# Attention over a cached K and V, gated with a small MLP: where gelu is kept, how the last K and V loads are ordered, and the form of the last product

## The chip, the core and the metric

The kernel runs on one core of one Trainium2 chip. Its time is the device time of one execution in microseconds; the figure of a kernel is the median of several runs. Five engines work side by side: TensorE (PE, with its weight loads listed as PEld), VectorE (DVE), ScalarE (ACT), GpSimd (POOL) and SyncE (SP), which here issues nearly all DMA transfers. Sixteen DMA engines move the data from memory (HBM) into the on-chip memory.

## What is computed

One token attends to a cache of 65,536 positions. There are 16 query heads and 8 K/V heads of width 256; two query heads share one K/V head. Beside that a small MLP works on the same input row, and a scalar gate mixes the two. Cut to what matters:

```python
def reference(A_x, A_k_cache, A_v_cache, A_wq, A_wo, B_x, B_w1, B_b1, B_w2, B_b2, gate_w):
    x = A_x                                              # [1, 1, 448], bf16 like all inputs
    g = _sigmoid((x * gate_w).sum(-1, keepdims=True))    # one number
    q = (x @ A_wq) as 16 heads of 256
    scores = q . k * 256 ** -0.5                         # k, v: [8, 65536, 256], each used by 2 heads
    a = softmax(scores) . v, all heads joined (4096) @ A_wo      # [1, 1, 448]
    h = _layernorm(x)
    u = _gelu(h[d] * w1[f] + b1[f])                      # [448, 1792], tanh form
    b = u @ w2 + b2                                      # [448]
    return g * a + (1 - g) * b
```

The caches are 256 MiB each, so 512 MiB have to be read once; wq and wo are 3.5 MiB each.

## The kernel before

**Blocks.** The cache of one K/V head is cut into four blocks of 16,384 positions, which makes 32 blocks, `n` from 0 to 31; `L` is 31. In a block, partition `p` holds 128 consecutive positions (its rows `j`). K lies in two tiles `k_tiles[0]` and `k_tiles[1]` of 64 rows each (4 MiB each), V in one tile `vt` of 128 rows (8 MiB). There is one buffer of each, so a load waits until the data before it has been read.

**One block.** `score_block` (L350) makes 32 steps `t`: four f32 transposes on TensorE (L327), which turn K rows into columns two bf16 at a time, and one copy by DVE (L332) from PSUM into `kT`. Four PSUM tiles `tps` are used in turn. Steps 0 to 15 read the first K tile, 16 to 31 the second; eight groups `i` of four steps each are followed, two and three steps later, by score matmuls (L341). `softmax` (L380) takes the block's maximum, joins it with the running one (L383 to L395), makes the exponentials on ScalarE (L399), the correction factor `al` (L404), transposes the exponentials into `pT` (L407) and updates the running sum `lsum` (L409). `pv_block` (L376) multiplies V by `pT` in 64 matmuls (L367) with 4 columns of `pT` stationary and 512 elements of V moving, and `accumulate` (L415) adds the product to `acc`, scaled by `al`. After four blocks `head_end` (L455) divides, collects `acc` into two columns per head (L439), and projects them with wo (L450) into a row `a_acc`.

**Order.** The helper `seq` chains the instructions of each engine in the order in which the program writes them, so each queue runs in that order. SyncE's queue, which issues the loads: wq, K of block 0, then for each block `n` V of `n` and the two K halves of `n + 1`; wo goes between V of block 0 and K of block 1 (L477). For `n` = 30 (L470) both K halves of block 31 come ahead of V of block 30. In block 31 (L482) the order is: all score steps, then `load_v_last`, then the products of block 30, `accumulate(30)`, `base` (the row of everything but the last head's share, L486), and then the softmax of block 31.

**The small MLP.** `gel`, the 14 x 448 gelu values per partition, lies in a part of `vt` (L100), which V of block 0 fills later. ScalarE writes it (L238); `mixer_tail` (L288), called after step 11 of block 0, reads it with 14 matmuls (L291) and makes `rest`, the MLP's share times one minus the gate. The gate's sum, its exponential and its reciprocal (L246 to L248, L279 to L282) stand ahead of block 0 in the queues of DVE and ScalarE.

**The end.** V of block 31 goes into the K tiles as they come free: `load_v_last` (L121) issues rows 0 to 63, 64 to 95, and then the last 32 rows in four pieces, each of which takes the same columns of two groups of 16 rows (`pairs`). Products of all but the last two columns of these pairs are made in the usual form (L507 to L513) and accumulated, `collect(fst, False)` (L515) gathers them, and the last four rows' products are made with V stationary (L519): 128 x 128 of V as weights, two columns of `pT` moving. Two multiplications by `rdv` (one over the sum) give `oT`, `project` makes the row, one DVE instruction (L528) multiplies by the gate and adds `base`, and one transfer of 896 bytes stores it (L532).

Of the kernel before, what the change touches and what calls it, by code (L numbers as in the profile page):

```python
# [8 lines left out]
FP32 = mybir.dt.float32  # L9
# [14 lines left out]
NI = VP // NJ  # L24
TAIL = 2


@with_exitstack
def kernel(
# [28 lines left out]
    def seq(ins):  # L58
# [40 lines left out]
    wq_t = vt[:, 48:56, :].rearrange("p a b -> p (a b)")  # L99
    gel = vt[:, 56:56 + 25, :].rearrange("p a b -> p (a b)")[:, 0:NF * D].rearrange(  # L100
        "p (b n) -> p b n", b=NF
    )

# [10 lines left out]

    def load_v(n):
        seq(nc.sync.dma_start(out=vt[:, :, :], in_=rows(A_v_cache, n)))

    def pairs(ap):
        return ap.rearrange("p (i j) d -> p i j d", i=2)

    def load_v_last(n):  # L121
        src = rows(A_v_cache, n)
        seq(nc.sync.dma_start(out=k_tiles[0][:, :, :], in_=src[:, 0:KP, :]))
        seq(nc.sync.dma_start(out=k_tiles[1][:, 0:32, :], in_=src[:, KP:KP + 32, :]))
        for j0, j1 in ((0, 8), (8, 12), (12, NJ - TAIL), (NJ - TAIL, NJ)):
            seq(nc.sync.dma_start(
                out=pairs(k_tiles[1][:, 32:64, :])[:, :, j0:j1, :],
                in_=pairs(src[:, KP + 32:VP, :])[:, :, j0:j1, :],
            ))
# [107 lines left out]
    for b in range(NF):  # L237
# [3 lines left out]
        ))  # L241
    zt = work.tile([1, D], FP32)
    z = const.tile([1, 1], FP32)
    ez = const.tile([1, 1], FP32)
    gate = const.tile([1, 1], FP32)
    seq(nc.vector.tensor_tensor(out=zt[:], in0=xf[0:1, :], in1=gw[:], op=ALU.mult))  # L246
    seq(nc.vector.tensor_reduce(out=z[:], in_=zt[:], op=ALU.add, axis=AXIS.X))
    seq(nc.scalar.activation(out=ez[:], in_=z[:], func=ACT.Exp, scale=-1.0))  # L248


# [24 lines left out]
    for i in range(1, NI):  # L275
        seq(nc.vector.tensor_copy(
            out=qpad[:, :, :, i, i * REP:(i + 1) * REP], in_=qpad[:, :, :, 0, 0:REP]
        ))
    seq(nc.vector.tensor_scalar(  # L279
        out=gate[:], in0=ez[:], scalar1=1.0, scalar2=None, op0=ALU.add  # L280
    ))
    seq(nc.vector.reciprocal(out=gate[:], in_=gate[:]))  # L282

    y_sb = const.tile([1, D], FP32)
    b2f = const.tile([1, 1], FP32)
    rest = const.tile([1, D], FP32)

    def mixer_tail():  # L288
        y_ps = hd_ps[0:1, 0:D]
        for b in range(NF):  # L290
            seq(nc.tensor.matmul(  # L291
                y_ps, lhsT=w2b[:, b:b + 1], rhs=gel[:, b, :], start=(b == 0), stop=(b == NF - 1)
            ))
        seq(nc.vector.tensor_copy(out=b2f[:], in_=b2b[:]))
        seq(nc.vector.tensor_scalar(  # L295
            out=y_sb[:], in0=y_ps, scalar1=b2f[0:1, 0:1], scalar2=None, op0=ALU.add
        ))
        seq(nc.vector.tensor_scalar(
            out=rest[:], in0=y_sb[:], scalar1=gate[0:1, 0:1], scalar2=None, op0=ALU.mult
        ))  # L300
        seq(nc.vector.tensor_tensor(out=rest[:], in0=y_sb[:], in1=rest[:], op=ALU.subtract))
# [17 lines left out]
    base = const.tile([1, D], FP32)  # L319
    res = const.tile([1, D], BF16)  # L320
    state = {"t": 0}
# [27 lines left out]

    def score_block(n, between=None):  # L350
        due = []
        for t, (i, quarter) in enumerate((i, q) for i in range(NI) for q in range(4)):
# [3 lines left out]
            if quarter == 3:  # L356
                due.append((t + 2, (i, 0)))
                due.append((t + 3, (i, 1)))
            if between is not None and t == 11:
                between()  # L360
        while due:
            scores(n // NB, *due.pop(0)[1])

    def pv(ip, j0, j1, v, first, final, end=NJ):
        for jj in range(j0, j1):
            grp = jj % 4
            seq(nc.tensor.matmul(  # L367
                pv_ps[32 * grp:32 * grp + 2 * REP, :, :],
                lhsT=pT[:, 32 * jj + 2 * REP * ip:32 * jj + 2 * REP * (ip + 1)],
                rhs=pairs(v)[:, :, jj, :],  # L370
                start=(first and jj < 4),
                stop=(final and jj >= end - 4),
                tile_position=(0, 32 * grp),
            ))

    def pv_block():  # L376
        for ip in range(NI // 2):
            pv(ip, 0, NJ, vt[:, 32 * ip:32 * (ip + 1), :], ip == 0, ip == NI // 2 - 1)

# [85 lines left out]

    L = NBLK - 1
    for n in range(NBLK):
        score_block(n, mixer_tail if n == 0 else None)
        if n < L:
            if n == L - 1:  # L470
                load_k(L, 0)
                load_k(L, 1)
                load_v(n)
            else:
                load_v(n)
                if n == 0:
                    seq(nc.sync.dma_start(  # L477
                        out=wo_sb[:], in_=A_wo.rearrange("(h r2 par) n -> r2 h par n", r2=128, par=2)
                    ))
                load_k(n + 1, 0)  # L480
                load_k(n + 1, 1)
        if n == L:  # L482
            load_v_last(L)
            pv_block()
            accumulate(n - 1)
            seq(nc.vector.scalar_tensor_tensor(  # L486
                out=base[:], in0=a_acc[:], scalar=gate[0:1, 0:1], in1=rest[:],
                op0=ALU.mult, op1=ALU.add,
            ))
        softmax(n)  # L490
        if n < L - 1:
            if n % NB == NB - 1:
                denominators()
            pv_block()
            accumulate(n)
            if n % NB == NB - 1:
                head_end(n // NB)


    seq(nc.vector.tensor_scalar(  # L500
        out=lsv[:], in0=val[:], scalar1=lsum[:, 0:1], scalar2=None, op0=ALU.mult
# [4 lines left out]
    seq(nc.vector.reciprocal(out=rdv[:], in_=hd_ps[:, 456:456 + REP]))  # L506
    for ip in range(2):  # L507
        pv(ip, 0, NJ, k_tiles[0][:, 32 * ip:32 * (ip + 1), :], ip == 0, False)
    pv(2, 0, NJ, k_tiles[1][:, 0:32, :], False, False)
    v_end = k_tiles[1][:, 32:64, :]  # L510
    pv(3, 0, 8, v_end, False, False)
    pv(3, 8, 12, v_end, False, True, NJ - TAIL)
    pv(3, 12, NJ - TAIL, v_end, False, True, NJ - TAIL)  # L513
    accumulate(L)
    collect(fst, False)  # L515
    for jj in range(NJ - TAIL, NJ):
        for e in range(2):
            for c in range(2):
                seq(nc.tensor.matmul(  # L519
                    o_ps[c],  # L520
                    lhsT=pairs(v_end)[:, e, jj, :].rearrange("p (d c) -> p c d", c=2)[:, c, :],
                    rhs=pT[:, 32 * jj + 2 * REP * 3 + REP * e:32 * jj + 2 * REP * 3 + REP * (e + 1)],
                    start=False, stop=(jj == NJ - 1 and e == 1),
                ))
    for c in range(2):
        seq(nc.vector.tensor_tensor(out=oT[:, c, :], in0=o_ps[c], in1=rdv[:], op=ALU.mult))  # L526
    project(HKV - 1)
    seq(nc.vector.scalar_tensor_tensor(  # L528
        out=res[:], in0=hd_ps[0:1, 0:D], scalar=gate[0:1, 0:1], in1=base[:],
        op0=ALU.mult, op1=ALU.add,  # L530
    ))
    seq(nc.sync.dma_start(out=out[0, 0].rearrange("(o n) -> o n", o=1), in_=res[:, :]))  # L532

# [29 lines left out]
```

## Time and profile before

| | |
|---|---|
| median of 3 runs | 1304.83 us (1304.53 to 1305.51) |
| the profiled execution's own time | 1304.43 us |
| its span, first to last instruction | 1302.6 us |
| mean granted TensorE clock | 0.848 of full speed |
| PE busy | 993.0 us (76%), 8553 matmuls |
| DVE busy | 755.6 us (58%) |
| ACT busy | 42.7 us (3%) |
| read from HBM | 544.22 MB, 418 GB/s over the span |

The profile is of one execution. Its page gives busy times, the span in 40 equal slices (busy tenths, clock, DMA share and GB/s), the DMA queues, the chain of work that ended last, the costliest groups of instructions and the DMA issues. From the trace come views of a stretch: windows with busy time per engine, a timeline, and the list of who waited for whom. In a timeline line stand start, duration, engine, source line and operation; in brackets the idle time ahead of it and what ended it. "SPq" is SyncE's queue of DMA issues.

### The profile page before, as it was taken

The page shows a single profiled execution, that of the slowest core. Times are in us where ns is not written, and L with a number is a line of the kernel's source. Part 1 is how long each engine was busy: PE and PEld are TensorE (multiplying, and loading weights), DVE is VectorE, ACT ScalarE, POOL GpSimd, SP SyncE. Part 2 cuts the span into 40 slices and gives each one's busy share as a digit, 9 for nine tenths or more (in the row PEclk, how much of TensorE's full clock was granted, in tenths as well). Part 3 has the DMA queues.
Part 4 walks back from the last instruction along what each step waited for, and adds up shares of the span by engine and source line. Part 5 has one row for each costly group of instructions (what it writes and reads, how often), then busy time and mean ns, then how long its engine had stood idle before and what let it go on. Part 6 is the DMA issues. An engine that isn't in the chain of part 4 may idle for free.

```text
span 1302.6 us, 19720 instructions
## 1 busy us (share of the span) xinstructions
PE 993.0 (76%) x8553; PEld 642.7 (49%) x8553; DVE 755.6 (58%) x1358; ACT 42.7 (3%) x107; POOL 4.2 (0%) x7
## 2 busy tenths in 40 slices
PE   3757787877877877687877787977788776888795
PEld 3434445544445545455544455544455544455562
DVE  3545567655566655566655567654567545566581
ACT  4000000000000000000000000000000000000000
POOL 1000000000000000000000000000000000000000
PEclk9877888978889887888878889887889878889786
DMA  8799999999999999999999999999999999999697
GB/s 371 323 435 445 415 430 430 440 436 424 425 432 432 438 431 434 417 432 434 435 437 425 430 427 433 432 443 422 431 427 431 429 422 437 425 428 430 273 420 291
DMA packets 18079, 545.49 MB, mean 419 GB/s; under 512 B 2117, under 2 KB 4680, under 8 KB 5320
## 3 DMA queue, kind: packets, MB, share of 16 engines
q1 hardware_dynamic: 17554, 544.22, 97.5%
q8 instruction: 67, 1.10, 0.3%
q14 instruction: 20, 0.16, 0.0%
q10 hardware_dynamic: 438, 0.01, 0.0%
HBM read 544.22 MB, written 0.00 MB: 418 GB/s over the span
## 4 chain that ended last, share of the span: by engine, by line
DMA 67%; PE 30%; DVE 2%; ACT 1%; issue 0%; ACTq 0%
DMA kn<-in_A_k_cache_dram 64%; PE tps L327 24%; PE sc_ps L341 6%; DMA kn<-in_A_v_cache_dram 2%; DVE kT L332 1%; DMA b1b<-in_B_b_dram 1%; ACT vt L238 1%; PE hd_ps L291 0%; PE hd_ps L450 0%; ACT L248 0%; PE hd_ps L439 0%; PE sm_ps L439 0%; DVE acc L417 0%; DVE rmax L383 0%; DVE y_sb L295 0%
## 5 line engine op out<-in xcount | busy, mean ns | idle before, releaser
L332 DVE COPY kT<-tps 128x1024 bf16<-128x1024 bf16 x1024 | 648.0, 685 | 184.2 <-PE tps L327 183.3
L327 PE MATMUL tps<-ident_f,kn 128*128 128x128 f32 x4096 | 610.6, 299 | 113.9 <-DMA kn<-in_A_k_cache_dram 107.0
L327 PEld LDWEIGHTS tps<-ident_f,kn 128*128 128x128 f32 x4096 | 493.0, 152 | 236.4 <-DMA kn<-in_A_k_cache_dram 124.1
L367 PE MATMUL pv_ps<-vt,pT 128*4 128x512 bf16 x1984 | 179.1, 540 | 89.7 <-DMA vt<-in_A_v_cache_dram 82.1
L341 PE MATMUL sc_ps<-kT,qpad 128*32 128x512 bf16 x2048 | 202.4, 395 | 26.1 <-DVE kT L332 25.6
L367 PEld LDWEIGHTS <-pT 128*4 128x4 bf16 x2046 | 61.8, 111 | 202.6 <-issue 144.1
L417 DVE SCALAR_TENSOR_TENSOR acc<-acc,al,pv_ps 128x512 f32<-128x512 f32 x24 | 17.9, 748 | 170.9 <-PE pv_ps L367 170.9
L341 PEld LDWEIGHTS <-qpad 128*32 128x32 bf16 x2048 | 52.9, 93 | 109.8 <-issue 101.7
L399 ACT ACTIVATE p_sb<-sc_ps,nb 128x512 bf16<-128x512 f32 x32 | 22.0, 687 | 1228.8 <-DVE nb L395 1228.8
L422 DVE COPY acc<-pv_ps 128x512 f32<-128x512 f32 x8 | 5.5, 692 | 61.7 <-PE pv_ps L367 61.7
L407 DVE STREAM_TRANSPOSE pT<-p_sb 128x512 bf16<-128x512 bf16 x32 | 22.8, 711 | 28.9 <-ACT p_sb L399 28.9
L383 DVE TENSOR_REDUCE rmax<-sc_ps 128x1 f32<-128x512 f32 x32 | 22.1, 691 | 22.8 <-PE sc_ps L341 22.8
L384 PE MATMUL sm_ps<-ident_f,rmax 128*1 128x128 f32 x32 | 8.6, 270 | 26.7 <-DVE rmax L383 26.7
L392 PE MATMUL sm_ps<-mrun,ones_f 1*128 1x2 f32 x64 | 15.2, 304 | 14.2 <-DVE mrun L391 11.7
L384 PEld LDWEIGHTS sm_ps<-ident_f,rmax 128*1 128x1 f32 x32 | 2.5, 79 | 43.1 <-DVE rmax L383 43.1
L392 PEld LDWEIGHTS sm_ps<-mrun,ones_f 1*128 1x128 f32 x64 | 12.4, 240 | 20.3 <-DVE mrun L391 16.3
L395 DVE CUSTOM_DVE_ANT_0 junk<-sm_ps,nval 128x2 f32<-128x2 f32 x32 | 5.1, 159 | 18.1 <-PE sm_ps L392 18.1
L425 PE MATMUL hd_ps<-lsum,same 128*128 128x1 f32 x14 | 3.9, 348 | 13.8 <-DVE lsum L409 13.8
L450 PE MATMUL hd_ps<-wo_sb,oT 128*1 128x448 bf16 x32 | 11.4, 463 | 0.2 <-DVE oT L526 0.2
L425 PEld LDWEIGHTS hd_ps<-lsum,same 128*128 128x128 f32 x14 | 3.3, 293 | 14.4 <-DVE lsum L409 14.4
L385 DVE TENSOR_REDUCE mnew<-sm_ps 1x2 f32<-1x64 f32 x24 | 5.1, 212 | 8.7 <-PE sm_ps L384 8.7
L238 ACT ACTIVATE vt<-h_bc,b1f,w1f 128x448 bf16<-128x448 f32 x14 | 9.2, 747 | 5.6 <-DVE h_bc L233 5.6
(92 smaller groups left out, 107.5 us busy)
## 6 DMA issues: line engine op xcount, KB each, us to landing
kn<-in_A_k_cache_dram SPq DMA_DIRECT2D x63, 4096.0 KB, 26.9
kn<-in_A_k_cache_dram SPq DMA_DIRECT2D x2, 2048.0 KB, 12.6
kn<-in_A_v_cache_dram SPq DMA_DIRECT2D x1, 4096.0 KB, 26.2
wo_sb<-in_A_wo_dram SPq DMA_DIRECT2D x1, 3584.0 KB, 32.3
vt<-in_A_wq_dram SPq DMA_DIRECT2D x1, 3072.0 KB, 10.3
kn<-in_A_v_cache_dram SPq DMA_DIRECT2D x1, 2048.0 KB, 25.7
kn<-in_A_v_cache_dram SPq DMA_DIRECT2D x1, 1024.0 KB, 24.7
vt<-in_A_wq_dram SPq DMA_DIRECT2D x1, 512.0 KB
```

The lines of the kernel that those rows point to most:

```text
L238: seq(nc.scalar.activation(out=gel[:, b, :], in_=h_bc[:], func=ACT.Gelu_apprx_tanh, scale=w1f[:, b:b + 1], bias=b1f[:, b:b + 1],))
L327: seq(nc.tensor.transpose(tp[:, jj * 128:(jj + 1) * 128], k_tiles[i // 4][:, i % 4 * NJ + quarter * 4 + jj, :].bitcast(FP32), ident_f[:, :],))
L332: seq(nc.vector.tensor_copy(out=kT_tiles[i % 2][:, quarter * 4:(quarter + 1) * 4, :, :].rearrange("p j n c -> p (j n c)"), in_=tp[:, :].bi ...
L341: seq(nc.tensor.matmul(sc_ps[32 * a:32 * (a + 1), :], lhsT=qpad[:, c, g, i, :], rhs=kT_tiles[i % 2][:, :, 32 * a:32 * (a + 1), c], start=( ...
L367: seq(nc.tensor.matmul(pv_ps[32 * grp:32 * grp + 2 * REP, :, :], lhsT=pT[:, 32 * jj + 2 * REP * ip:32 * jj + 2 * REP * (ip + 1)], rhs=pair ...
L383: seq(nc.vector.tensor_reduce(out=rmax[:], in_=sc_ps[:, :], op=ALU.max, axis=AXIS.X))
L384: seq(nc.tensor.transpose(sm_ps[0:1, 0:128], rmax[:, 0:1], ident_f[:, :]))
L392: seq(nc.tensor.matmul(sm_ps[:, 128:128 + REP], lhsT=ones_f[0:1, :], rhs=mrun[0:1, :], start=True, stop=True))
L399: seq(nc.scalar.activation(out=p_sb[:, :], in_=sc_ps[:, :], func=ACT.Exp, scale=scale, bias=nb[:, 0:1], accum_out=den[:, 0:1],))
L407: seq(nc.vector.transpose(out=pT[:, :], in_=p_sb[:, :]))
L417: seq(nc.vector.scalar_tensor_tensor(out=acc[:], in0=acc[:], scalar=al[:, 0:1], in1=pv_ps[:, :, :], op0=ALU.mult, op1=ALU.add,))
L450: seq(nc.tensor.matmul(a_ps, lhsT=oT[:, c, r:r + 1], rhs=wo_sb[:, g * REP + r, c, :], start=(r == 0 and c == 0), stop=(r == REP - 1 and c ...
```

## The change

Five things are changed.

1. `gel` lies in a part of `wo_sb` instead of `vt`. wo's load is issued after both K halves of block 1. Within wo, the two rows of a pair are now indexed `c`, as in the same memory order as before.
2. The gate's sum and exponential are made after step 8 of block 0 (`gate_sum`), its reciprocal at the head of `mixer_tail`, and `mixer_tail` is called after step 20 instead of 11.
3. For block 30, SyncE issues V's first half, K's first half of block 31, V's second half, K's second half of block 31.
4. In block 31 the products of block 30, `accumulate`, `base` and a new copy of the gate on all partitions (`gcol`) are made after step 17. `load_v_last` issues rows 0-63, 64-95, 96-111, 112-119, 120-123, 124-127, each contiguous.
5. All 128 rows of the last V are stationary: 256 matmuls with 128 x 128 of V as weights and two columns of `pT` moving, which add to `collect(esc, False)`; `esc` is `al` on the selected rows. The final result is made in columns: 112 partitions by 4, with wo's columns as weights, and `base` added by four f32 matmuls ahead; the gate is multiplied into `rdv`. The store writes 112 pieces of 8 bytes.

```diff
@@ gelu @@
-    gel = vt[:, 56:56 + 25, :].rearrange("p a b -> p (a b)")[:, 0:NF * D].rearrange(
-        "p (b n) -> p b n", b=NF
-    )
+    gel = wo_sb[:].rearrange("p h c n -> p (h c) n")[:, 0:NF, :]
...
+    LAST = ((0, 64), (64, 96), (96, 112), (112, 120), (120, 124), (124, 128))
+
     def load_v_last(n):
-        src = rows(A_v_cache, n)
-        seq(nc.sync.dma_start(out=k_tiles[0][:, :, :], in_=src[:, 0:KP, :]))
-        seq(nc.sync.dma_start(out=k_tiles[1][:, 0:32, :], in_=src[:, KP:KP + 32, :]))
-        for j0, j1 in ((0, 8), (8, 12), (12, NJ - TAIL), (NJ - TAIL, NJ)):
+        for j0, j1 in LAST:
             seq(nc.sync.dma_start(
-                out=pairs(k_tiles[1][:, 32:64, :])[:, :, j0:j1, :],
-                in_=pairs(src[:, KP + 32:VP, :])[:, :, j0:j1, :],
+                out=k_tiles[j0 // KP][:, j0 % KP:(j1 - 1) % KP + 1, :],
+                in_=rows(A_v_cache, n)[:, j0:j1, :],
             ))
...
+    def gate_sum():
+        seq(nc.vector.tensor_tensor(out=zt[:], in0=xf[0:1, :], in1=gw[:], op=ALU.mult))
+        seq(nc.vector.tensor_reduce(out=z[:], in_=zt[:], op=ALU.add, axis=AXIS.X))
+        seq(nc.scalar.activation(out=ez[:], in_=z[:], func=ACT.Exp, scale=-1.0))
...
+    def products(n):
+        pv_block()
+        accumulate(n)
+
+    def project_base():
+        seq(nc.vector.scalar_tensor_tensor(
+            out=base[:], in0=a_acc[:], scalar=gate[0:1, 0:1], in1=rest[:],
+            op0=ALU.mult, op1=ALU.add,
+        ))
+        seq(nc.tensor.matmul(
+            sm_ps[:, 200:201], lhsT=ones_f[0:1, :], rhs=gate[0:1, 0:1], start=True, stop=True
+        ))
+        seq(nc.vector.tensor_copy(out=gcol[:], in_=sm_ps[:, 200:201]))
+
+    def before_last():
+        products(L - 1)
+        project_base()
+
     for n in range(NBLK):
-        score_block(n, mixer_tail if n == 0 else None)
...
+        if n == 0:
+            score_block(n, {8: gate_sum, 20: mixer_tail})
+        elif n < L:
+            score_block(n)
+        else:
+            score_block(n, {17: before_last})
+        if n < L - 1:
+            load_v(n)
+            load_k(n + 1, 0)
+            load_k(n + 1, 1)
+            if n == 0:
+                seq(nc.sync.dma_start(
+                    out=wo_sb[:], in_=A_wo.rearrange("(h p c) n -> p h c n", p=128, c=2)
+                ))
+        elif n == L - 1:
+            load_v(n, 0, KP)
+            load_k(L, 0)
+            load_v(n, KP, VP)
+            load_k(L, 1)
+        else:
+            load_v_last(L)
...
+    f_ps = tps[0][0:D // NCOL, 0:NCOL]
+    for k in range(NCOL):
+        seq(nc.tensor.matmul(
+            f_ps[:, k:k + 1], lhsT=base[0:1, :].rearrange("o (m k) -> o k m", k=NCOL)[:, k, :],
+            rhs=ones_f[0:1, 0:1], start=(k == 0), stop=False, skip_group_check=True,
+        ))
+    seq(nc.vector.tensor_scalar(
+        out=esc[:], in0=fst[:], scalar1=al[:, 0:1], scalar2=None, op0=ALU.mult
+    ))
...
+    collect(esc, False)
+    for j in range(VP):
+        i, jj = divmod(j, NJ)
+        for c in range(2):
+            seq(nc.tensor.matmul(
+                o_ps[c],
+                lhsT=k_tiles[j // KP][:, j % KP, :].rearrange("p (d c) -> p c d", c=2)[:, c, :],
+                rhs=pT[:, 32 * jj + REP * i:32 * jj + REP * (i + 1)],
+                start=False, stop=(j == VP - 1),
+            ))
     for c in range(2):
         seq(nc.vector.tensor_tensor(out=oT[:, c, :], in0=o_ps[c], in1=rdv[:], op=ALU.mult))
-    project(HKV - 1)
-    seq(nc.vector.scalar_tensor_tensor(
-        out=res[:], in0=hd_ps[0:1, 0:D], scalar=gate[0:1, 0:1], in1=base[:],
-        op0=ALU.mult, op1=ALU.add,
-    ))
-    seq(nc.sync.dma_start(out=out[0, 0].rearrange("(o n) -> o n", o=1), in_=res[:, :]))
+    for c in range(2):
+        for r in range(REP):
+            for k in range(NCOL):
+                seq(nc.tensor.matmul(
+                    f_ps[:, k:k + 1],
+                    lhsT=wo_sb[:, HQ - REP + r, c, :].rearrange("p (m k) -> p k m", k=NCOL)[:, k, :],
+                    rhs=oT[:, c, r:r + 1],
+                    start=False, stop=(r == REP - 1 and c == 1), skip_group_check=True,
+                ))
+    seq(nc.vector.tensor_copy(out=res[:], in_=f_ps))
+    seq(nc.sync.dma_start(out=out[0, 0].rearrange("(m k) -> m k", k=NCOL), in_=res[:, :]))
```

## The prediction

> **What bounds the kernel now.** First the page's 40 slices (32.6 us each), then windows of the trace around the slices that stand out.
>
> ```profile
> DMA  8799999999999999999999999999999999999697
> GB/s 371 323 435 445 415 430 430 440 436 424 425 432 432 438 431 434 417 432 434 435 437 425 430 427 433 432 443 422 431 427 431 429 422 437 425 428 430 273 420 291
> ```
>
> The DMA engines are busy nearly throughout at about 430 GB/s; issues of V in blocks 2 to 29 lie 39.21 us apart (116.11 to 1174.83 in 27 steps), or 9.8 us for a 4 MB half. Bytes do not change, so only the slices 323, 273 and 291 can. Windows (start:end, length, busy time of five engines, TensorE clock, DMA share, GB/s), then SyncE's waits and its issues (start, duration):
>
> ```profile
> 30.00:39.00 9.00, 9.00 (x59) 5.21 (x56) 5.21 (x10) 0.00 (x0) 0.00 (x0) 1.00 0.04 14
> 1206.00:1216.00 10.00, 6.02 (x64) 2.00 (x64) 1.56 (x3) 0.26 (x2) 0.00 (x0) 0.66 1.01 434
> 1216.00:1226.00 10.00, 7.21 (x42) 6.22 (x43) 4.84 (x7) 0.00 (x0) 0.00 (x0) 0.66 0.49 210
> 1226.00:1232.00 6.00, 6.00 (x56) 4.41 (x55) 5.47 (x9) 0.00 (x0) 0.00 (x0) 1.00 0.01 5
> ```
> ```profile
> SPq L116 <- PE hd_ps L291: 24.7, 1, 24.7
> ```
> ```profile
> 38.60 0.33 SPq L116 DMA_DIRECT2D vt<-in_A_v_cache_dram  x1
> 1231.49 0.33 SPq L110 DMA_DIRECT2D kn<-in_A_k_cache_dram  x1
> 1242.70 0.89 SPq L116 DMA_DIRECT2D vt<-in_A_v_cache_dram  x1
> ```
>
> Gap one: V of block 0 waits until L291 has read gelu out of `vt`; nothing moves from 30 to 39 us. Gap two: V of block 30 stands behind both K halves of block 31, which wait for block 30's transposes. But from 1216 to 1226 half of the DMA engines (0.49) still work: some engines run about 10 us behind the others at this point. A transfer has landed when its slowest engine is done, so for the late engines gap two is only the 4.4 us between the last packet's end at 1228.0 and the next one at 1232.4.
>
> The end (timeline):
>
> ```profile
> 1275.23 5.39 PE L367 MATMUL pv_ps<-vt,pT 128*4 128x512 bf16 x64 [4.35 <-DMA vt<-in_A_v_cache_dram]
> 1281.94 0.67 DVE L383 TENSOR_REDUCE rmax<-sc_ps 128x1 f32<-128x512 f32 x1
> 1285.55 0.18 DVE L409 SCALAR_TENSOR_TENSOR lsum<-lsum,al,den 128x1 f32<-128x1 f32 x1
> 1295.92 1.01 PE L439 MATMUL hd_ps<-fst,acc 128*128 128x2 f32 x4 [0.84 <-DVE acc L417]
> 1297.65 0.17 PE L519 MATMUL hd_ps<-pT,kn 128*128 128x2 bf16 x1
> 1297.83 0.17 PE L519 MATMUL sm_ps<-pT,kn 128*128 128x2 bf16 x1
> 1298.22 1.65 PE L450 MATMUL hd_ps<-wo_sb,oT 128*1 128x448 bf16 x4 [0.23 <-DVE oT L526]
> 1300.61 0.33 SPq L532 DMA_DIRECT2D out_dram<-res  x1
> ```
>
> Today the last V byte lands at 1295.4 and 7.2 us of work follow: the end is bound by data.
>
> **The change part by part.** All sums are in the profiled execution's time: span 1302.6, time 1304.43, which is 0.4 below the median 1304.83.
>
> *Gelu, gate and y.* V of block 0 now waits only for the wq matmuls, whose last starts at 15.8, so it is queued long before the engines run dry. Mean over all engines the gap is worth (430 - 14) / 430 x 9 = 8.7 us; for the one engine that ends last (33.0, next packet 39.55) it is 6.5. Between 32 and 34 us only 0.03 MB move, so nearly all engines are close to the upper end: I take 8.0. The gate's two DVE operations and the wait for Exp leave the head of DVE's queue, where today the kT copies start only at 27.26. This buys block 0 some us that DMA hides. wo moves behind both K halves of block 1; all three are issued by about 46 us, before V of block 0 is through (31 + 19.6 = 50.6). Today the K issue behind wo holds SyncE for 19.9 us (from 41.46); in the new order V of block 1 can be held likewise, but K halves and wo, 28 us of transfers, stand ahead of it. Cost 0; without this cover up to the 8 us again.
>
> *K and V halves alternating.* V's first half of block 30 is issued when L367 of block 29 has read it (today 1215.1 at the latest, before the early engines run dry at 1216). The late engines then work through without a stop: block 30's K ends at 1228.0 - 8.0 = 1220.0, and V half, K half, V half, K half take 4 x 9.8: K's second half of block 31 lands at 1259.2, plus 0.3 for the completion. The early engines do stop, some 6 us before block 30's t = 15 frees the first K tile (1231.49 - 8.0 = 1223.5), which costs nothing as long as the others are later.
>
> *The products of block 30 at t = 17.* Here TensorE becomes the bound. Step 16 needs that second K half, so everything queued behind it, products of block 30 included, waits until 1259.5, although V of block 30 is there ten us earlier. From 1259.5: steps 16 and 17, 8 transposes at the slow clock 1.8 (L327 after a wait: 24 in 5.4 us), scores 0.6, products 5.4 (row above): 1267.3. Behind them DVE does acc 0.75, base 0.67 and the new gcol copy 0.2: 1268.9. Fourteen steps are left at 0.677 (today 16 steps from 1231.49 to 1242.32 = 10.83). TensorE runs four tiles ahead, so step 31 ends at 1268.9 + 0.69 + 9 x 0.677 + 0.43 = 1276.1. Who waits for it: V pieces of block 31 that go into K's second tile. Rows 64 to 96 of each partition go out after step 23, about 1270.7, first bytes 0.95 later (1231.49 to 1232.44), so the engines stop from 1269.0 to 1271.7, and V ends 9.8 us on, 1281.5 to 1282.5 with the small pieces.
>
> *End of block 31.* Step 31 to rmax 1.45 (1242.32 to 1243.77): 1277.6. rmax to lsum's end 3.8 (1281.94 to 1285.73): 1281.4. esc and lsv 0.5, the ones matmul L503 0.6: 1282.5. The four new f32 matmuls of base are like L392 (0.4 to 0.6 each), and fit into the 2.2 us that TensorE waits for lsv today. collect: 1.1 at full clock (195.04 to 196.1), 1.75 here: 1284.3. By then all of V is on the chip.
>
> *256 pairs of weight load and matmul.* The nearest rows are exactly this shape: L519 does 8 in 1297.65 to 1297.83, and L257 with L264 do their last 125 in 12.45 to 15.77: 26 ns and 26.6 ns. 256 x 26.6 = 6.8 us: 1291.1. Upper bound 104 ns a pair, the busy time of each such weight load, if none overlapped: 26.6 us.
>
> The Trainium skill, page "TensorE: Matmul & The Clock Gate", section "LDWEIGHTS (loading the stationary operand)", puts a load at columns / 1.2 ns: 107 ns for 128 columns, which would make these 256 loads 27.3 us and the kernel about 13 us slower than before. Its section "Weight-path perf modes" knows a faster load for full 128-column weights, measured at about twice the speed: 13.7 us, and a kernel as fast as before. The trace's 26.6 ns is half of that again, at both clocks; the trace decides.
>
> *Output in columns.* oT 0.4 (1297.83 to 1298.22). Sixteen matmuls with 112-column weights are not in the trace: at least 26.6 ns each (0.4), at most the f32 transposes' 107 (12 in 1.29: 1.7); by the nearer bf16 rows 0.9, plus 0.2 drain: 1292.6. The copy of 112x4 0.2 instead of L528's 0.67. The store was 2.0 from issue to the end; with 112 pieces of 8 bytes 2.0 to 2.6 (the 128 pieces of 28 bytes into w1b took 0.37 to issue against 0.32 to 0.52 for single rows): 2.2. End 1295.0.
>
> Sum: span 1302.6 to 1295.0, minus 7.6; time 1304.43 - 7.6 = 1296.8, and 0.4 more on the median's scale: **1297**. Put differently, the front's 8 us stay; what gap two gives, the end takes back.
>
> **Rivals.** (1) Both gaps return in full by the GB/s row: 8.7 and, for 1216 to 1232, 16 - (210 x 10 + 5 x 6) / 430 = 11.0, and DMA still ends the kernel: 1304.8 - 19.7 = 1285. For it: the engines are the bound in 37 slices. Against: the half-busy window, and that block 31's products stand behind its last K half. 11%. (2) Slower: the pairs do not overlap. Place: between collect and oT, nothing beside them. From 26.6 + (1304.8 - 1297) / 256 = 57 ns a pair the kernel is slower than before; at 104 it takes 1297 + 256 x 0.0774 = 1317. For it: the loads' 104 ns; L519 shows only 8, with loads pulled ahead. Against: 125 in a row. 7%. (3) The front does not close, because wo's descriptors hold SyncE and the engines run dry later: 8 us back, 1305. For: the 19.9 us issue. Against: the 28 us of queued transfers. 5%.
>
> **How the numbers follow.** My case has 77%, with its own range 1292 to 1302: front 6.5 to 8.7, collect at 1.1, base matmuls not hidden (2), wo matmuls and store at their ends, and up to 3 us should instruction supply slow 512 instructions in 7 us. The range 1290 to 1302 leaves out most of the three rivals. Faster by over 0.2% (2.6 us, about what this kernel's measurement can tell from nothing): 0.86; within 0.2%: 0.05 (rival 3, my upper tail); slower: 0.09.
>
> **What would show it.** Front: no window under 400 GB/s between 30 and 45. Gap two: none in which the whole queue is empty at 1216 to 1232, but a dent of half-busy engines. End: SyncE's issue of V rows 64 to 96 waits on L325; TensorE's wait for K before step 16 of block 31; products after it; 256 pairs in about 7 us that wait for no DMA. Wrong if the pairs wait for V (then data is the bound and rival 1 nearer), if they take over 50 ns, or if the lag between DMA engines is gone by 1220.

## The result, and the profile after

The changed kernel takes 1295.51 us (median; 1294.80 to 1296.10, four runs) where the kernel before takes 1304.68 beside it (1304.32 to 1305.51): a ratio of 0.9929, 95% interval 0.9911 to 0.9946, so 9.2 us less. The prediction was 1297.0. Its profiled execution has a span of 1293.7 us (predicted 1295.0) and took 1295.6. The sum came out right to 1.5 us. The experiments below show that two errors, of 4.7 and 3.4 us, nearly cancelled in it. (Short names from here on: K31 is K of block 31, V30 is V of block 30, and so on.)

The 40 slices on the page of the changed kernel:

```profile
DMA  9999999999999999999999999999999999999993
GB/s 406 426 426 432 437 425 429 434 437 436 433 426 431 433 439 435 427 434 428 431 437 434 438 424 428 436 434 432 436 429 424 439 423 442 418 427 436 392 402 134
```

The dent of the second slice (323 GB/s before) is gone, and that of slice 38 is 392 in place of 273. The last slice, 134 in place of 291, is new: the end is no longer bound by data. The same windows as before the change (window, length, busy time of PE, PEld, DVE, ACT, POOL, granted clock, DMA share, GB/s):

```profile
30.00:39.00 9.00, 6.07 (x35) 3.94 (x36) 3.88 (x9) 0.00 (x0) 0.00 (x0) 0.81 1.08 465
1206.00:1216.00 10.00, 10.00 (x82) 7.75 (x80) 8.86 (x15) 0.00 (x0) 0.00 (x0) 0.89 0.88 380
1216.00:1226.00 10.00, 10.00 (x92) 7.14 (x88) 9.10 (x15) 0.00 (x0) 0.00 (x0) 1.00 0.92 372
1226.00:1232.00 6.00, 2.89 (x27) 1.52 (x23) 3.33 (x9) 0.74 (x3) 0.00 (x0) 1.00 1.02 438
```

Gap one has closed (465 GB/s where there were 14). Of gap two only a dent is left: 0.88 and 0.92 of the engines are busy in the two windows, and at the deepest 0.66 (1216 to 1218). A dent was predicted, though a deeper one, of half-busy engines. SyncE's waits (line, what it waited for: us in total, times, longest):

```profile
SPq L114 <- PE hd_ps L253: 1.7, 1, 1.7
...
SPq L582 <- DMA out_dram<-res: 3.0, 1, 3.0
```

V of block 0 now waits 1.7 us for the wq matmuls, where it waited 24.7 us for the reader of gelu. The second line is the last instruction's wait for the store to be complete; in the same view of the kernel before it was

```profile
SPq L558 <- DMA out_dram<-res: 0.5, 1, 0.5
```

The end in the timeline of the changed kernel, lines picked out (start, duration, engine, line, operation; in brackets the idle time and its releaser; `rmax` is the maximum of the block's scores, with which its softmax begins):

```profile
1254.83 1.94 PE L325 MATMUL tps<-ident_f,kn 128*128 128x128 f32 x8 [7.67 <-DMA kn<-in_A_k_cache_dram]
1257.11 4.80 PE L365 MATMUL pv_ps<-vt,pT 128*4 128x512 bf16 x64
1261.97 0.75 DVE L415 SCALAR_TENSOR_TENSOR acc<-acc,al,pv_ps 128x512 f32<-128x512 f32 x1 [4.46 <-PE pv_ps L365]
1266.55 5.74 SPq L123 DMA_DIRECT2D kn<-in_A_v_cache_dram  x5
1273.38 0.69 DVE L381 TENSOR_REDUCE rmax<-sc_ps 128x1 f32<-128x512 f32 x1 [0.72 <-PE sc_ps L339]
1277.01 0.18 DVE L407 SCALAR_TENSOR_TENSOR lsum<-lsum,al,den 128x1 f32<-128x1 f32 x1
1286.89 0.17 PE L538 MATMUL sm_ps<-pT,kn 128*128 128x2 bf16 x1
1287.28 1.73 PE L549 MATMUL tps<-oT,wo_sb 128*112 128x1 bf16 x16 [0.22 <-DVE oT L545]
1289.05 0.16 DVE L555 CAST res<-tps 112x4 bf16<-112x4 f32 x1 [1.75 <-PE tps L549]
1289.23 0.36 SPq L556 DMA_DIRECT2D out_dram<-res  x1
```

TensorE waits 7.67 us for the second K half of block 31, then makes the products of block 30; the rest is one chain of TensorE and DVE to the store. From the store's issue (1289.23) to the span's end (1293.7) it is 4.5 us; before it was 2.0. The groups of instructions between 1279.5 and the end (count, busy us, mean ns, idle before) settle what the 256 pairs of a weight load and a matmul cost (the "pairs" from here on):

```profile
L538 PEld LDWEIGHTS <-kn 128*128 128x128 bf16 x256 | 7.1, 105 | 0.0
```

256 loads of 105 ns each lie within 7.1 us: they overlap, one pair in 26.6 ns (1280.09 to 1286.89), with no wait for a DMA.

### The profile page after: what moved, and what is told of

Same layout as the page of the kernel before. It is cut to its first block, busy times and chain, and to the rows that moved or that the text cites. A ratio compares the mean times of both kernels' runs of the same rounds, so it can differ in the third digit from the quotient of the medians.

```text
span 1293.7 us, 20135 instructions
## 1 busy us (share of the span) xinstructions
PE 984.2 (76%) x8761; PEld 644.0 (50%) x8761; DVE 753.0 (58%) x1360; ACT 42.8 (3%) x107; POOL 4.2 (0%) x7
## 4 chain that ended last, share of the span: by engine, by line
DMA 66%; PE 31%; DVE 2%; issue 0%; ACT 0%; ACTq 0%; DVEq 0%
DMA kn<-in_A_k_cache_dram 63%; PE tps L325 23%; PE sc_ps L339 5%; DMA vt<-in_A_v_cache_dram 3%; DVE kT L330 1%; PE pv_ps L365 1%; PE sm_ps L538 0%; PE hd_ps L538 0%; PE tps L549 0%; PE hd_ps L437 0%; ACT p_sb L397 0%; DVE pT L405 0%; PE hd_ps L448 0%; DVE rmax L381 0%; PE sm_ps L437 0%
## 5 line engine op out<-in xcount | busy, mean ns | idle before, releaser
L325 PEld LDWEIGHTS tps<-ident_f,kn 128*128 128x128 f32 x4096 | 488.0, 151 | 231.1 <-issue 115.6
L365 PEld LDWEIGHTS <-pT 128*4 128x4 bf16 x1984 | 59.0, 110 | 200.4 <-issue 140.6
L390 PE MATMUL sm_ps<-mrun,ones_f 1*128 1x2 f32 x64 | 14.4, 292 | 14.1 <-DVE mrun L389 11.7
L437 PE MATMUL hd_ps<-esc,acc 128*128 128x2 f32 x32 | 5.5, 275 | 6.3 <-DVE acc L415 6.0
L437 PEld LDWEIGHTS hd_ps<-esc,acc 128*128 128x128 f32 x32 | 4.8, 212 | 9.9 <-DVE acc L415 9.6
```

The source lines that it names most:

```text
L325: seq(nc.tensor.transpose(tp[:, jj * 128:(jj + 1) * 128], k_tiles[i // 4][:, i % 4 * NJ + quarter * 4 + jj, :].bitcast(FP32), ident_f[:, :],))
L365: seq(nc.tensor.matmul(pv_ps[32 * grp:32 * grp + 2 * REP, :, :], lhsT=pT[:, 32 * jj + 2 * REP * ip:32 * jj + 2 * REP * (ip + 1)], rhs=pair ...
L390: seq(nc.tensor.matmul(sm_ps[:, 128:128 + REP], lhsT=ones_f[0:1, :], rhs=mrun[0:1, :], start=True, stop=True))
L437: seq(nc.tensor.matmul(o_ps[c], lhsT=acc[:, e, :].rearrange("p (d c) -> p c d", c=2)[:, c, :], rhs=weights[:, e, :], start=(e == 0), stop= ...
```

## The experiments

Twelve kernels ran, on several chips; each time stands beside runs of the kernel before on the same chip, so ratios are what is compared across groups.

### The front and the end, each alone

**Front alone:** the kernel before with gelu in wo's place, wo behind K of block 1, gate and y (the 14 matmuls of `mixer_tail`) inside block 0; loads, products and end as before.

```diff
-    gel = vt[:, 56:56 + 25, :].rearrange(...)
+    gel = wo_sb[:].rearrange("p h c n -> p (h c) n")[:, 0:NF, :]
...
```

> The kernel before with the front's edits alone (gelu in wo's place, gate and y inside block 0, wo behind K of block 1); loads, products and end as before. My theory (what gap two gives, the end takes back): nearly all of the gain is here, 1291 to 1295 us, gap two still open. The trace of after stands 9.7 us ahead at block 1 and 13.6 at block 29; if the growth comes with the front it is seen here too, and the time is 1291 to 1292; if it was chance of one execution, 1295. Rival (both gaps count by their lost bytes, the end edits bring half of the gain): 1299 to 1301.

Measured: 1295.20, ratio 0.9931 (0.9916 to 0.9946), as fast as the whole change. Gap two is there in full (windows of this run):

```profile
1216.00:1226.00 10.00, 10.00 (x93) 7.22 (x90) 8.88 (x15) 0.00 (x0) 0.00 (x0) 1.00 0.26 82
```

**End alone:** the changed kernel with the front of the kernel before.

```diff
-    gel = wo_sb[:].rearrange("p h c n -> p (h c) n")[:, 0:NF, :]
+    gel = vt[:, 56:56 + 25, :].rearrange(...)
...
```

> The changed kernel with the front of before (gelu in vt, gate at the head, y at step 11, wo ahead of K of block 1). My theory: the late DMA engines gain only the 4.4 us of gap two, and the wait at step 16, the 256 pairs and the store of 8-byte pieces take that back or more: 1304 to 1309 us, no gain. Rival (end edits bring half): 1298 to 1301.

Measured: 1304.96, ratio 1.0008 (0.9998 to 1.0017). So far this is the prediction's sentence: the front's gain stays, the end gains nothing. But the traces held something that neither theory had. In the packet records, the kernel with the end alone runs level with the kernel before at block 1 and is 4.6 us ahead of it at block 29, although no edit of the end acts before block 30. The changed kernel's lead over the kernel before (by how much earlier the last packet of a block's V ends) grows likewise, from 9.6 to 13.5 us; that of the front alone does not (9.3 to 8.4).

### The products of block 30, and the row

**Products at step 15**, ahead of the wait for the second K half.

```diff
-            score_block(n, {17: before_last})
+            score_block(n, {15: before_last})
```

> The changed kernel with the products of block 30 after step 15 instead of 17 of block 31, so that they run while TensorE waits for the last K half (1247 to 1254.8). My theory (the chain from that landing is the bound, products stand in it): 5 to 6 us less, 1290 us. Rival (the last V's data are the bound): at most 2 us less, 1294 to 1295.5, and the pairs then wait for DMA.

Measured: 1292.02, ratio 0.9910 (0.9895 to 0.9925), by the medians 3.5 us under the changed kernel, by the ratios 2.5 (their intervals overlap; the pair of runs on one chip below is clearer); less than expected. Timeline:

```profile
1246.66 3.62 PE L365 MATMUL pv_ps<-vt,pT 128*4 128x512 bf16 x64
...
1254.90 1.61 PE L325 MATMUL tps<-ident_f,kn 128*128 128x128 f32 x8 [4.31 <-DMA kn<-in_A_k_cache_dram]
```

The products fit into the wait and are shorter too (3.62 us against 4.80): TensorE comes to them from work and not from a 7.67 us wait, and the granted clock in the window around them is 1.00 where it was 0.75. K lands at the same time; the wait shrinks to 4.31, and the store goes out 4.55 us earlier (1284.68 for 1289.23).

**Row store**: the last head projected into a row and stored as one piece of 896 bytes.

```diff
-    res = const.tile([D // NCOL, NCOL], BF16)
+    res = const.tile([1, D], BF16)
...
-    seq(nc.vector.tensor_copy(out=res[:], in_=f_ps))
-    seq(nc.sync.dma_start(out=out[0, 0].rearrange("(m k) -> m k", k=NCOL), in_=res[:, :]))
+    project(HKV - 1)
+    seq(nc.vector.tensor_tensor(out=res[:], in0=hd_ps[0:1, 0:D], in1=base[:], op=ALU.add))
+    seq(nc.sync.dma_start(out=out[0, 0].rearrange("(o n) -> o n", o=1), in_=res[:, :]))
```

> The changed kernel, but the last projection makes a row as before (4 matmuls with oT stationary, base added by DVE) and one piece of 896 bytes is stored. My theory (the 112 pieces of 8 bytes complete 2.4 us later, 16 matmuls and the small copy are worth about the 4 and the larger one): 2 to 2.5 us less, 1293.3 us. Rival (the end's latency does not depend on the pieces): 1295.5 to 1296.5.

Measured: 1298.52, ratio 0.9958 (0.9941 to 0.9974), 3 us slower than the changed kernel. Yet the store did what was expected of it (SyncE's waits):

```profile
SPq L570 <- DMA out_dram<-res: 0.6, 1, 0.6
```

From issue (1295.10) to the span's end (1297.2) it is 2.1 us. What had gone wrong lay 35 us ahead of it: the second K half of block 31 came at 1259.98 and not at 1254.83.

```profile
1259.98 1.94 PE L325 MATMUL tps<-ident_f,kn 128*128 128x128 f32 x8 [7.31 <-DMA kn<-in_A_k_cache_dram]
```

This kernel's lead over the kernel before does not grow (8.8 us in block 1, 8.4 in block 29), like that of the front alone.

### Why the blocks have two speeds

What the kernels of one speed have in common is where the K and V tiles begin in a partition. The line of the change that moves them is not among those shown ahead of the prediction (`gcol` is new, as said there):

```diff
-    res = const.tile([1, D], BF16)
+    res = const.tile([D // NCOL, NCOL], BF16)
+    gcol = const.tile([128, 1], FP32)
```

`res` lies ahead of the K and V tiles in the partition; it takes 896 bytes there in the kernel before and 8 in the changed one, and all that follows moves. In the kernel before and with the front alone K begins at byte 66112, 64 over a multiple of 256; with the row store at 66144, 96 over; in the changed kernel, with the end alone and with the products at step 15 at 65280, a multiple of 256. (The move is 832 bytes and not 888, as `gcol` lies there too and not every tile takes just its own bytes.) Two kernels change nothing but the size of `res`.

**Before, aligned:**

```diff
-    res = const.tile([1, D], BF16)
+    res_w = const.tile([1, D + 96], BF16)
+    res = res_w[:, 0:D]
```

> The kernel before with one change: the tile res takes 1088 bytes of a partition where it took 896, so that the K and V tiles behind it begin at byte 66304 of the partition, a multiple of 256, and not at 66112, which is 64 over one. Alignment theory: each block of 16.8 MB takes 39.09 to 39.11 us (kernels so far that began at a multiple of 256: 39.087, 39.105, 39.112) where the kernel before takes 39.25; over some 28 blocks that is 4 to 5 us, so 1299.5 to 1301. Rival, that the block periods differed for another reason (the earlier start of the transfers, the order of the last ones, or chance): 1304.5, within 1.

**After, shifted:**

```diff
-    res = const.tile([D // NCOL, NCOL], BF16)
+    res_w = const.tile([D // NCOL, 48], BF16)
+    res = res_w[:, 0:NCOL]
```

> The changed kernel with one change: res takes 96 bytes of a partition where it took 8, so that the K and V tiles begin at byte 65344, 64 over a multiple of 256, as in the kernel before. Alignment theory: block period 39.25 to 39.28 us, the second half of K31 lands near 1259.5, 1299 to 1300.5. Rival: 1295.5, within 1.

Measured: the kernel before, aligned, 1297.60, ratio 0.9958 (0.9944 to 0.9971); the changed kernel, shifted, 1300.62, ratio 0.9974 (0.9965 to 0.9983). Both as the alignment theory had it, the first even 2 us faster than its range. Of the 6.9 us by which its span is shorter, 4.6 stand at block 29; the rest comes behind it, and no run takes it apart. In the second the last K half lands 5.0 us later than in the changed kernel:

```profile
1259.83 1.94 PE L326 MATMUL tps<-ident_f,kn 128*128 128x128 f32 x8 [8.07 <-DMA kn<-in_A_k_cache_dram]
```

SyncE's issues of V in blocks 2 and 29, 27 blocks apart, show the pace. The kernel before, aligned:

```profile
116.09 0.33 SPq L116 DMA_DIRECT2D vt<-in_A_v_cache_dram  x1
...
1170.86 0.33 SPq L116 DMA_DIRECT2D vt<-in_A_v_cache_dram  x1
```

The changed kernel, shifted:

```profile
107.65 0.33 SPq L114 DMA_DIRECT2D vt<-in_A_v_cache_dram  x1
...
1166.33 0.33 SPq L114 DMA_DIRECT2D vt<-in_A_v_cache_dram  x1
```

(1170.86 - 116.09) / 27 = 39.07 us, and 39.21 as in the kernel before (the prediction's 39.21). By the ends of V's last packets in blocks 1 and 29 the fourteen traces fall into two groups without overlap:

| K begins over a multiple of 256 by | kernels | us a block |
|---|---|---|
| 0 | 10 | 39.09 to 39.12 |
| 64 (three kernels), 96 (one) | 4 | 39.25 to 39.28 |

In V of blocks 1 to 29 the median 64 KB packet takes 2418 ns in the first group and 2420 in the second, the mean 2428 to 2429 and 2433 to 2436. That is all there is to see of it, at most 0.3% a packet. By the table a block differs by 0.16 us, and 28 blocks by 4.5. All tiles behind `res` move together; that it is the K and V tiles whose place counts is read from the packets of their loads, and no run moves them alone.

The Trainium skill, page "DMA: Bandwidth & Descriptors", section "How a descriptor splits into AXI transactions", says that a transaction must start at a 256-byte boundary, so that a descriptor that starts elsewhere can cost a transaction more. By that an estimate for a packet of 64 KB would be 257 transactions in place of 256, 0.4%. The page's examples are about bytes that are read; here the source is the same and the destination moves. The direction and the size agree with the rows above; whether this is the mechanism no run here shows, nor whether a multiple of 128 would do.

### What the end costs, with the alignment held

**Row, aligned:** the row store with `res` padded to 1056 bytes.

```diff
-    res = const.tile([1, D], BF16)
+    res_w = const.tile([1, D + 80], BF16)
+    res = res_w[:, 0:D]
```

> The changed kernel with the result in a row and stored as one piece of 896 bytes, as the earlier run of the row, but with res padded so that the K and V tiles begin at a multiple of 256. Alignment theory: the landing of K31 goes back to 1254.9, the store still takes 2.1 us from issue to end where the changed kernel's took 4.5, and its row costs some 0.3 us more than the columns did: 1293.0 to 1294.0. Rival, that the row is slower for itself: 1298.5, within 1.

**Products at step 15, row, aligned:** the same with `{15: before_last}`.

> The same with the products of block 30 at step 15 of the last block instead of step 17, in the wait for the second half of K31. If the two gains are independent (3.5 us by the products, some 2 by the store): 1289.2 to 1290.5. Rival, that one hides the other: 1291.5 to 1292.5.

Measured: 1293.57, ratio 0.9922 (0.9908 to 0.9935), and 1289.17, ratio 0.9890 (0.9875 to 0.9906). The row gives 1.9 us on the changed kernel by the medians and 0.9 by the ratios, whose intervals overlap; what shows it is the trace. Its store goes out at 1289.37, as late as in the changed kernel (1289.23), and the span ends 2.1 us behind it and not 4.5. The products give 4.4 us on top in the same group. So the gains add, and the loss of the first row store came from the alignment. The stores of the two:

```profile
1289.37 0.32 SPq L545 DMA_DIRECT2D out_dram<-res_w  x1
```
```profile
1284.87 0.33 SPq L545 DMA_DIRECT2D out_dram<-res_w  x1
```

**Front alone, aligned:** the kernel with the front alone, so with the whole end of the kernel before, and a padded `res`.

```diff
-    res = const.tile([1, D], BF16)
+    res_w = const.tile([1, D + 96], BF16)
+    res = res_w[:, 0:D]
```

> The kernel before with the front edits of the change (gelu in wo's place, wo behind K1, gate and y inside block 0) and with res padded to 1088 bytes, so that the K and V tiles begin at a multiple of 256; the end is that of the kernel before: order of the last loads, moving V, row. Theory that the edits of the end cost time: the padding alone gave 7.0 us on the kernel before (1304.6 to 1297.6), the front alone 9.1 (1304.3 to 1295.2), and the two add: 1288 to 1289.5, 6 to 7 us faster than the changed kernel, which has the same front and the same alignment. Rival, that the edits of the end are worth about nothing, as they looked against the unaligned kernel before: 1294.5 to 1296.5.

Measured: 1289.79, ratio 0.9893 (0.9878 to 0.9908). This kernel has the front and the alignment of the changed one, and is faster than it by 5.7 us (4.7 by the ratios): the edits of the end cost time. It is level with the kernel of the row and the products at step 15 (0.9893 against 0.9890). So the place of the products and the columns with their store make up the whole cost, and what is left of the end's edits, gap two included, comes to nothing together as far as these intervals tell; what the new order of loads is worth by itself no run shows. Its windows and timeline:

```profile
1204.00:1214.00 10.00, 8.77 (x64) 7.02 (x65) 7.14 (x11) 0.00 (x0) 0.00 (x0) 0.83 0.43 184
1214.00:1220.00 6.00, 6.00 (x56) 4.42 (x55) 5.33 (x10) 0.00 (x0) 0.00 (x0) 1.00 0.43 142
```
```profile
1260.94 5.24 PE L366 MATMUL pv_ps<-vt,pT 128*4 128x512 bf16 x64 [4.65 <-DMA vt<-in_A_v_cache_dram]
...
1285.95 0.32 SPq L531 DMA_DIRECT2D out_dram<-res_w  x1
```

Gap two is wide open, and the store still goes out 3.3 us earlier than in the changed kernel (1289.23) and takes 2.0 us instead of 4.5.

### The order of the last loads

**V whole first:** V30 whole, then both K halves of block 31; no alternating.

```diff
-            load_v(n, 0, KP)
-            load_k(L, 0)
-            load_v(n, KP, VP)
-            load_k(L, 1)
+            load_v(n)
+            load_k(L, 0)
+            load_k(L, 1)
```

> The changed kernel with the last loads in the order V30 whole, K31 first half, K31 second half, so without alternating. As many bytes stand ahead of K31's second half. Theory of the late engines (the queue of the latest engines never runs dry, so the order ahead of it is nothing to the landing): it lands at 1254.8 as before, within 0.5; but K31's first half lands later, so that steps 0 to 15 are done some 2.6 us after that: 1297.5 to 1299. Rival, that the alternation itself costs transfer time: the second half lands 2 to 3 us earlier, 1294 to 1296.

Measured: 1295.23, ratio 0.9935 (0.9918 to 0.9951), no different from the changed kernel. The time is that of the rival, the mechanism is not: the second K half's last packet ends at 1254.29, and at 1254.38 in the changed kernel, as the theory of the late engines has it. The price that was expected was missed, because a late first half is not followed by a second wait (timeline):

```profile
1245.09 5.38 PE L325 MATMUL tps<-ident_f,kn 128*128 128x128 f32 x24 [13.67 <-DMA kn<-in_A_k_cache_dram]
...
1258.91 3.62 PE L365 MATMUL pv_ps<-vt,pT 128*4 128x512 bf16 x64
```

TensorE works through from 1245.09, and makes the products in 3.62 us and not in 4.80. They begin 1.8 us later and rmax comes only 0.6 later (1274.00).

**K before V's second half:** V30 first half, K31 whole, V30 second half; products of the first half right after the softmax of block 30, the rest at step 27; row, aligned.

```diff
             load_v(n, 0, KP)
             load_k(L, 0)
-            load_v(n, KP, VP)
             load_k(L, 1)
+            load_v(n, KP, VP)
...
         softmax(n)
+        if n == L - 1:
+            for ip in (0, 1):
+                pv(ip)
```

> The changed kernel with the last loads in the order V30 first half, K31 first half, K31 second half, V30 second half; the products of block 30 with its first half right after the softmax of block 30, those with its second half, the accumulation and the base at step 27 of block 31; the result in a row, res padded to a multiple of 256. Theory that the wait for K31's second half is what the end pays: it lands some 9.5 us earlier (4.2 MB fewer ahead of it), near 1245, step 31 ends near 1262.5, the pairs begin near 1270 and end behind the landing of V31 near 1276.5: 1281.5 to 1283.5. Rival, that the transfers of V31 bound the end: they land no earlier than in the run with the products at step 15 (1273.8) and the tail behind them is as long, 1286 to 1289.

Measured: 1283.54 (1282.01 to 1283.70), ratio 0.9843 (0.9828 to 0.9858): at the upper edge of what was expected, and the fastest kernel here, 12 us under the changed one (11 by the ratios). Timeline:

```profile
1234.52 3.58 PE L366 MATMUL pv_ps<-vt,pT 128*4 128x512 bf16 x32 [1.88 <-DVE pT L406]
1256.92 1.90 PE L366 MATMUL pv_ps<-vt,pT 128*4 128x512 bf16 x32
1263.45 0.69 DVE L382 TENSOR_REDUCE rmax<-sc_ps 128x1 f32<-128x512 f32 x1 [0.74 <-PE sc_ps L340]
...
1279.68 0.32 SPq L550 DMA_DIRECT2D out_dram<-res_w  x1
```

No wait for K is left in block 31, and rmax comes 9.9 us earlier than in the changed kernel. The rival's premise held all the same: the last bytes of V31 end at 1273.91, no earlier than with the products at step 15 (1273.83). But the pairs begin at 1270.16 now, wait for no DMA and are through 3 us behind the last bytes, so the tail is shorter: 5.8 us from there to the store's issue where it was 11.0.

### The gate

**Gate at the head:** the gate's five operations back at the head, y at step 11; gelu stays in wo's place.

```diff
-            score_block(n, {8: gate_sum, 20: mixer_tail})
+            score_block(n, {11: mixer_tail})
```

> The changed kernel with the gate's three head operations and its two last ones back at the head, where the kernel before has them, and y back at step 11 of block 0 instead of step 20; gelu stays in wo's place. Theory that the transfers cover all of it: the first V is issued at 15.5 us as before and the transfers of the front have no gap, so 1295.5 within 0.5. Rival, that the gate's operations at the head hold up the queries and with them the first transposes far enough to leave the queue dry once (the gap of the kernel before was 7 us): 1297 or more.

Measured: 1295.10, ratio 0.9940 (0.9926 to 0.9953), no difference from the changed kernel that these intervals can tell. SyncE's issues:

```profile
15.70 0.33 SPq L114 DMA_DIRECT2D vt<-in_A_v_cache_dram  x1
41.27 11.78 SPq L108 DMA_DIRECT2D kn<-in_A_k_cache_dram  x2
```

K of block 1 is issued 11.7 us later than in the changed kernel (29.57), but the queue still holds V of block 0 and does not run dry: 466 GB/s from 30 to 39.

## Why the prediction was right, point by point

The edits that the prediction weighed explain only part of the 9.2 us. By the ratios, in us of 1304.6: the front -9.0 (0.9931); the alignment -5.5 on the kernel before (0.9958), -5.9 on the changed one (0.9929 against 0.9974); the edits of the end +4.7 with the alignment held (0.9929 against 0.9893), +5.6 without it (0.9974 against 0.9931), +6.5 with it behind the old front (1.0008 against 0.9958). -9.0 - 5.5 + 4.7 makes -9.8 where -9.3 was measured.

| step of the prediction | predicted | measured |
|---|---|---|
| the front | -8.0 | -9.0 in time; lead of 9.6 us in block 1 |
| transfers between front and end | no term | lead grows by 3.9 us up to block 29 |
| late engines lose nothing in gap two | 0 | at most 0.9 us |
| TensorE resumes at step 16 | 1259.5 | 1254.83 |
| steps 16, 17, to the products | 2.4 us | 2.28 |
| products, acc, base, gcol | 7.0 us | 6.26 |
| from there to rmax | 8.7 us | 10.0 |
| rmax to the pairs | 6.7 us | 6.71 |
| 256 pairs | 6.8 us | 6.80 |
| oT and the 16 wo matmuls | 1.5 us | 2.16 |
| copy | 0.2 us | 0.18 |
| store to the span's end | 2.2 us | 4.47 |

**The front** was right in cause and some 1 us short. That V of block 1 would be held in SyncE's queue was right too:

```profile
59.63 13.07 SPq L114 DMA_DIRECT2D vt<-in_A_v_cache_dram  x1
```

Nothing starved meanwhile: in windows of 5 to 9 us from 30 to 74 us the engines moved 383 GB/s or more. That the place of the gate and of y is worth about nothing is shown by the run with them back in theirs.

**The missing term.** The step that failed is "Bytes do not change, so only the slices 323, 273 and 291 can". The bytes did not change, their addresses did. The cause is one line, the new shape of `res`, which the prediction took for an output format. Of the 4.7 us by which K's landing was missed, 3.9 are this growth and 1.6 the front (9.6 for 8.0), less 0.9 lost in gap two: with K of block 30 ending 13.5 us ahead of the kernel before (1228.0 - 13.5 = 1214.5), four halves of 9.78 and 0.3 give 1253.9, and TensorE resumed at 1254.83.

**Gap two.** That only the late engines decide was right: four halves behind the last of K30 come to within 0.9 us of the landing, although the others had paused. The order without alternating, with as many bytes ahead, landed K at the same time; and the kernel with gap two open and the old end is faster than the changed one all the same.

**The end.** "What gap two gives, the end takes back" was too kind. The end takes back more: the products behind the wait cost 2.5 to 4.4 us, and the columns with their store 1 to 2. The mechanism, TensorE behind the last K half, was the predicted one. Mis-sized were three terms. The store: 2.2 with bounds of 2.0 to 2.6, measured 4.47; the upper bound came from how long a load of 28-byte pieces took to issue, and that is a row neither for a write nor for its completion. The 16 wo matmuls: 1.73 us, the upper end of the bounds given (1.7), as much as the 1.65 us of the four row matmuls they replace. And the 14 steps to rmax, 1.3 us too short, because time for ten of DVE's copies was counted behind `gcol`, where fourteen follow it in the trace.

**The rivals.** The pairs overlapped to the predicted 26.6 ns. Both gaps' return in full did not come, and the front did close.

So the total was right by cancellation: 4.7 us too late at K's landing, 3.4 too early behind it (the rows of the table below that one), 1.3 together.

## What to carry to other kernels

In a kernel bound by transfers, compare the addresses of the big tiles before and after a change, not only the bytes: here a result tile smaller by 888 bytes was worth 5 to 6 us, more than half of what the front gave, and it made a good edit look bad (the row store: 3 us slower than the changed kernel unaligned, some 2 faster aligned). An edit that shows no gain alone should be run again with such a side effect held, because two effects of some 5 us hid each other here twice (the end alone against the kernel before, and the changed kernel against the front alone). And put work that is ready ahead of a wait, not behind it: the same 64 products, with the additions behind them, cost 2.5 to 4.4 us more when they stood two steps later.

## What the runs showed of the hardware that was not expected

- K and V tiles that begin at a multiple of 256 bytes in the partition load 16.8 MB in 39.09 to 39.12 us, those that begin 64 or 96 bytes over it in 39.25 to 39.28.
- 112 pieces of 8 bytes written to HBM take 4.5 us from issue to the end of the span in the changed kernel, and 4.7 to 5.1 in the five others that store them; one piece of 896 bytes takes 2.0 to 2.1. In the changed kernel the last small piece's packet ends at 1290.28, and the completion that the kernel waits for comes 2.5 us later (2.5 to 3.1 in the six); behind the piece of 896 bytes it comes 0.3 us later (first row store). The Trainium skill, page "DMA: Bandwidth & Descriptors", section "Specifications", puts the least transfer at full rate at 512 bytes and a read-modify-write below it; the runs agree in direction, and show no more of the cause.
- A weight load of 128 columns and its matmul take 26.6 ns in the run of 256, those of 112 columns 107 to 108 (1.73 us / 16), both at a granted clock of 0.50 in their windows. The first take every second element of V's rows, the second every fourth of wo's, so no run separates the width from the step.
- The sixteen DMA engines drift apart: V's first and last packets of a block start 1.6 us further apart than at an even pace in block 0 and 11.1 in block 29 of the changed kernel, much the same in all traces. This lag hides gap two. At the end it is the lag of one engine that counts: of the sixteen landings of K31's second half in the changed kernel seven come at 1248.4 to 1248.9, eight at 1251.2 to 1253.2, and the one that TensorE waits for at 1254.7. The cause stays open.
